# Second-layer products all 256 columns wide, with their moving operands 192 bytes beyond the weights modulo 256

## The chip, the core and the metric

The kernel runs on one core of one Trainium2 chip. The metric is the device time of one execution in microseconds, median of three runs. The core has a matrix engine (TensorE, PE in the profile, with its weight loads listed apart as PEld), VectorE (DVE), ScalarE (ACT), GpSimd (POOL) and a queue for transfers (SP). Tiles lie in on-chip memory of 128 partitions; an address below is the byte offset in a partition. Products are summed in PSUM.

## What is computed

Three stages follow each other. A gated scan over 768 steps for 4 batches and 8 heads gives 3072 rows of 256 numbers; a first layer of width 1536 with SiLU gating; a second layer of width 2048 with a squared ReLU:

```
y   = scan(x, a, B, C)                       # 3072 rows x 256
xn  = y / sqrt(mean(y*y) + 1e-6) * rms_g
r1  = (silu(xn @ w_gate) * (xn @ w_val)) @ w_out1     # 3072 x 256
h   = r1 @ w_in                              # 3072 x 2048
out = (s * relu(h)**2 + b) @ w_out           # 3072 x 256
```

## The kernel before, in words

Rows lie along the columns of tiles, features along partitions. Every full-precision number is kept as two float32r numbers, a high part and the rest (`split`, line 802: a copy on ACT that rounds, a subtraction on DVE). A product of two such pairs is three TensorE products, high x high, low weight x high, high weight x low (`three`, line 795). Each of the three names its own weights, so each comes with a weight load of 128 x 128.

The scan and the first layer share the first part of the program. The first layer goes over blocks of 384 or 512 rows (`NB`); its first block multiplies ten of its twelve feature tiles in plain float32 (`hidden1_plain`, line 849). The second layer starts at about 363 us and goes over six groups of 512 rows, each with 16 feature tiles taken in 8 pairs (`seven`, line 963). For one pair there are twelve h products: two feature tiles x two halves of the 256 inputs x three. Each has 512 columns (line 970). ACT then applies ReLU to the 512 columns of a PSUM bank and squares them; the columns are two halves of 256 rows, and the pair of features and the pair of halves go through seven products instead of eight: DVE forms sums and differences (`added`, `less`), each is split into `hi` and `lo`, and `seven_out` (line 993) makes 7 x 3 = 21 products of 256 columns with combined weights `w2c`, summed over the eight pairs into seven PSUM areas (called `acc` or `o` in the trace, according to the bank). These 21 products stand in TensorE's order two pairs behind the h products (`LAG`, line 51). After eight pairs the seven sums are put together (lines 1003 to 1025) and stored. ACT and DVE need the time of a pair for the work on the next.

The order on each engine is computed before anything is emitted: class `Plan` records every operation with an estimated duration (`price`, line 216) and its dependences (`touch`, line 182), lists them forward and backward, and emits each engine's instructions in the order found. For a float32r product it assumes n / 2.285 + 7 ns (line 231).

Where the tiles lie matters for the change. The weights `w2h` and `w2c`, the rows `x1h` and `x1l`, and `hi` and `lo` come from pools that follow each other in memory. Each buffer of these pools has a multiple of 256 bytes per partition (3072 for `w1h` and the `hi` and `lo` of `seven`, 4096 for the rows, 2048 for `w2h` and for the pool `hl`). So all of them, weights and moving operands, start at the same address modulo 256.

The buffers of the first layer's high weights, pool `wts` with 12 buffers, are used again in the second layer for `hi` and `lo`, four per pair, which repeats every three pairs.

Of the kernel before, what the change touches and what calls it, by code (L numbers as in the profile page):

```python
# [8 lines left out]
F32 = mybir.dt.float32  # L9
F32R = mybir.dt.float32r  # L10
# [9 lines left out]
P = 128  # L20
# [28 lines left out]
KEPT = max([t1 - t0 for parts in PARTS for _, t0, t1 in parts[1:]])  # L49
LAST = [max(c for c in range(NUNIT) if any(j == i for i, *_ in PARTS[c])) for j in range(NBLK)]  # L50
LAG = 2
F1 = 12
F2 = 16
PLAIN = 10
HALVES = 5
ORDER = [*range(PLAIN, F1), *range(PLAIN)]
N2 = 512
HALF = N2 // 2
DM = 256
SIZE = {F32: 4, F32R: 4, I32: 4, U32: 4, BF16: 2, I16: 2, U16: 2, I64: 8}  # L60
# [3 lines left out]
class Engine:  # L64
    def __init__(self, plan, name):
        self.plan, self.name = plan, name
# [5 lines left out]
class Plan:  # L72
# [21 lines left out]
    SWITCH = {"matmul": 0.24, "transpose": 0.15}  # L94
    LATE = 0.6
    PASSES = 3

    def __init__(self, nc):
        self.nc, self.ops, self.clock, self.pace = nc, [], 0.0, False
# [82 lines left out]
    def touch(self, op, ap, write):  # L182
        t = getattr(ap, "tensor", None)
        tag = getattr(t, "tag", None)
        if tag is None:
            return
        tag = str(tag)
        name = ap.name
        whole = "PSUM" in str(ap.space) or "DRAM" in str(ap.space)
        if name not in self.seen:  # L190
            self.seen[name] = []
            ring = self.rings.setdefault(tag, [])
            bufs = t.bufs or t.tag_meta.bufs
            self.before[name] = list(self.seen[ring[-bufs]]) if len(ring) >= bufs else []
            self.closed.update(ring[:1 - bufs] if bufs > 1 else ring)
            ring.append(name)
        for *_, o in self.before[name]:
            self.need(op, o)
        p0, p1, mask = (0, 128, self.banks(ap)) if whole else self.cover(ap)
        for w, q0, q1, m, o in self.seen[name]:  # L200
            apart = "PSUM" in str(ap.space) and o["eng"] != op["eng"]
            if (apart or (write or w) and m & mask) and q0 < p1 and p0 < q1:
                self.need(op, o)
        assert name not in self.closed, name
        self.seen[name].append((write, p0, p1, mask, op))

    def need(self, op, o):
# [137 lines left out]
    def issue(self, idle, warm):  # L345
# [13 lines left out]
        found = []  # L359
        for _ in range(self.PASSES):  # L360
            start, stop = self.forward(succs, late)
# [34 lines left out]
def scan_glu_relu2(ctx: ExitStack, tc: tile.TileContext, bc, xr, aa, cst, w1, w2, gn, sv, bv, out):  # L396
    nc = Plan(tc.nc)
    PS = bass.MemoryType.PSUM

    const = ctx.enter_context(tc.tile_pool(name="const", bufs=1))  # L400
    wts = ctx.enter_context(tc.tile_pool(name="wts", bufs=F1))
    wlo = ctx.enter_context(tc.tile_pool(name="wlo", bufs=F2))
    dram = ctx.enter_context(tc.tile_pool(name="dram", bufs=1, space=bass.MemoryType.DRAM))
    w2_p = ctx.enter_context(tc.tile_pool(name="w2", bufs=4))
# [8 lines left out]
    hl_p = ctx.enter_context(tc.tile_pool(name="hl", bufs=LAG + 1))  # L413
    res_p = ctx.enter_context(tc.tile_pool(name="res", bufs=1))
# [16 lines left out]
    warm = const.tile([P, 1], F32, name="warm")  # L431
    a_scr = dram.tile([2 * NUNIT, NH * AW], F32, name="a_scr")

    w1h = {m: wts.tile([P, 6, P], F32R, tag="w1h", name="w1h") for m in ORDER}
    w1f, w1l, w2f, w2h = {}, {}, {}, {}
    w2_sum = const.tile([P, 2, P], F32, name="w2_sum")

    def f32(t):
        return t.bitcast(F32)
# [256 lines left out]
            )  # L696

    rest = {}
    kept = const.tile([P, 2, 2, KEPT], F32, name="kept")

    def turn(units):
        for c in units:
            new_rows(BLOCK[c])
        bundled("t", units, turn_products)
        for c in units:
            tp = y_p[c % NPAIR][:, 1, 4 * R:4 * R + 2 * P].rearrange("p (k z r) -> p k z r", k=2, z=2)
            (j, t0, t1), *more = PARTS[c]
            place_rows(j, c, [tp[:, k, :, NST + t0:NST + t1] for k in range(2)])
            for j, t0, t1 in more:
                rest[j] = (c, kept[:, :, :, 0:t1 - t0])  # L710
                nc.vector.tensor_copy(out=rest[j][1], in_=tp[:, :, :, NST + t0:NST + t1])

    def turn_rest(j):
# [43 lines left out]
    def flat(t):  # L757
        return t.rearrange("p a b -> p (a b)")
# [3 lines left out]
    def words(out, src):  # L762
        nc.turns = True
        nc.sync.dma_start(out=out, in_=src)
        nc.turns = False
# [18 lines left out]
    def decode2(m):  # L784
        raw = w2_p.tile([P, 4 * P], I64, tag="w2", name="raw2")
        words(raw, w2[m])
        w2f[m] = w2f_p.tile([P, 4, P], F32, tag="w2f", name="w2f")
        decode(raw, flat(w2f[m]), 4 * P, nc.vector)
        if m:
            last = w2f[0][:, 2:4] if m == 1 else w2_sum  # L790
            nc.gpsimd.tensor_tensor(out=w2_sum, in0=last, in1=w2f[m][:, 2:4], op=ALU.add)

# [2 lines left out]
    def three(out, wh, wl, xh, xl, first, last):  # L795
        nc.pace = True
        nc.tensor.matmul(out=out, lhsT=wh, rhs=xh, start=first, stop=False)
        nc.tensor.matmul(out=out, lhsT=wl, rhs=xh, start=False, stop=False)
        nc.tensor.matmul(out=out, lhsT=wh, rhs=xl, start=False, stop=last)
        nc.pace = False  # L800
# [8 lines left out]
    o_t, x1_t, rows1 = {}, {}, {}  # L809
# [11 lines left out]
    def evac1(o, t, j):  # L821
        at, end = START[j], START[j + 1]
        for i in range(at // (2 * N2), (end - 1) // (2 * N2) + 1):
            if i not in rows1:
                rows1[i] = x1_p.tile([P, 2, 2 * N2], F32, tag="x1", name="rows1")
            lo, hi = max(at, 2 * N2 * i), min(end, 2 * N2 * (i + 1))
            nc.scalar.copy(out=rows1[i][:, t, lo - 2 * N2 * i:hi - 2 * N2 * i], in_=o[t][:, lo - at:hi - at])

    def split_rows(g):
        x1_t[g] = [w2_p.tile([P, 2, N2], F32R, tag="w2", name=f"x1{v}") for v in "hl"]  # L830
        split(rows1[g // 2][:, :, g % 2 * N2:(g % 2 + 1) * N2], *x1_t[g])

    def hidden1(j, m):
# [107 lines left out]
    def bias_products():  # L941
        ps = ps_y.tile([P, 2, 512], F32, tag="y", name="bias")
        ones = nc.nc.const_aps.tensor(1.0, (P, 2), F32)
        for t in range(2):
            nc.tensor.matmul(out=ps[:, t, 0:2], lhsT=w2_sum[:, t], rhs=ones, start=True, stop=True)
        nc.vector.tensor_scalar(out=minus_s, in0=s_sb, scalar1=-1.0, scalar2=None, op0=ALU.mult)
        for t in range(2):
            nc.vector.tensor_scalar_mul(bias_sb[:, t:t + 1], ps[:, t, 0:1], b_sb)

    def new_sums(j):  # L950
        n = HALF

# [10 lines left out]
    def seven(j, q):  # L963
        n = HALF
        (xh, xl), s = x1_t[j], []
        for i in range(2):
            m = 2 * q + i
            ps = ps_h.tile([P, 512], F32, tag="h", name="h")[:, :2 * n]
            for k in range(2):
                three(ps, w2h[m][:, 0, k], w2h[m][:, 1, k], xh[:, k], xl[:, k], k == 0, k == 1)  # L970
            t = s_p.tile([P, 2 * n], F32, tag="s", name="s")
            nc.scalar.activation(out=t, in_=ps, func=AF.Relu)
            nc.scalar.activation(out=t, in_=t, func=AF.Square)
            s.append(t.rearrange("p (s n) -> p s n", s=2))

        added = xt_p.tile([P, 3, n], F32, tag="xtl", name="added")
        less = xt_p.tile([P, 2, n], F32, tag="xth", name="less")
        hi, lo = ([wts.tile([P, 3, n], F32R, tag="w1h", name=f"{v}{k}") for k in range(2)] for v in ("hi", "lo"))
        hi2 = hl_p.tile([P, n], F32R, tag="hi", name="hi")
        lo2 = hl_p.tile([P, n], F32R, tag="lo", name="lo")  # L980
        split(s[0][:, 0], hi[1][:, 2], lo[1][:, 2])
        split(s[1][:, 1], hi2, lo2)
        nc.vector.tensor_tensor(out=added[:, 0], in0=s[0][:, 0], in1=s[1][:, 1], op=ALU.add)
        for i in range(2):
            nc.vector.tensor_tensor(out=added[:, 1 + i], in0=s[i][:, 0], in1=s[i][:, 1], op=ALU.add)
        split(added, hi[0], lo[0])
        nc.vector.tensor_tensor(out=less, in0=s[0], in1=s[1], op=ALU.subtract)
        split(less, hi[1][:, 0:2], lo[1][:, 0:2])
        parts = [(hi[1][:, 2], lo[1][:, 2]), (hi2, lo2)] + [(hi[0][:, k], lo[0][:, k]) for k in range(3)]
        parts += [(hi[1][:, k], lo[1][:, k]) for k in range(2)]  # L990
        pending.append(lambda: seven_out(j, q, parts))

    def seven_out(j, q, parts):
        n = HALF
        if q == 0:
# [31 lines left out]
    def drain(n):  # L1027
# [13 lines left out]
        out=ident, in_=ident, compare_op=ALU.not_equal, fill=1.0, base=0,  # L1041
# [3 lines left out]
    for z in range(2):  # L1045
        rows = slice(z * R, (z + 1) * R)
        nc.vector.tensor_copy(
            out=delta[rows, :, 0:CH], in_=ident[rows, None, z * R + NST:(z + 1) * R].to_broadcast([R, NH, CH])
# [3 lines left out]
    for u in range(4):  # L1052
        rows = slice(u * 32, (u + 1) * 32)
        nc.vector.tensor_copy(
            out=first_bc[rows, :, 0:NST], in_=ident[rows, None, u * 32:u * 32 + NST].to_broadcast([32, 2, NST])
# [66 lines left out]
    start = {(layer, j): i for i, (layer, j, m) in reversed(list(enumerate(plan)))}  # L1122
    marks = [(start[1, j], count[LAST[j]]) for j in range(1, NBLK)]
    for i, (layer, j, m) in enumerate(plan):
        at = i - start[layer, j]
# [101 lines left out]
```

## Time and profile before

| | us |
|---|---|
| median of 3 runs (lowest to highest) | 626.06 (625.53 to 626.33) |
| the profiled execution | 626.15 |
| its span, first to last instruction | 624.4 |
| TensorE busy | 614.7 |
| VectorE busy | 484.5 |
| ScalarE busy | 448.4 |
| GpSimd busy | 55.2 |

The profiled execution is 0.09 us above the median. The span leaves out 1.75 us ahead of the first and behind the last instruction. The granted TensorE clock was 0.999 of full speed over the span. A product's duration in the trace, such as 392 ns for 512 columns, holds its passage through the array, and the next product starts well before it ends. What a product costs is the distance from its start to the start of the next; the chain of waits shows that distance summed over a run of products.

### The profile page before, as it was taken

To read this page: it belongs to the slowest core of one execution; us is meant where nothing else is said; L and a number is where in the kernel's file an instruction comes from. 1 tells how busy PE (TensorE), PEld (TensorE's weight loads), DVE (VectorE), ACT (ScalarE), POOL (GpSimd) and SP (SyncE) were. 2 spreads that over 40 slices of the span, in tenths; PEclk is the share of its full clock that TensorE was granted. 3 is DMA by queue.
4 is the path that set the end of the run, shared out by engine and by line. 5 is a ranking of instruction groups with operands and counts; after the bars stand their busy time and mean duration, and the time that the engine had idled before them with its cause. 6 is when DMAs were issued, how large, how long until landed. Compare 5 with 4: busy or idle time off the path is not lost.

```text
span 624.4 us, 12905 instructions
## 1 busy us (share of the span) xinstructions
PE 614.7 (98%) x4937; PEld 544.2 (87%) x4937; DVE 484.5 (78%) x978; ACT 448.4 (72%) x945; POOL 55.2 (9%) x88
## 2 busy tenths in 40 slices
PE   9999999999999999999999999999999999999996
PEld 7886899999988888888889999999999999999985
DVE  7999965778856865685685678898897897987975
ACT  5797553766636653664665589898898998988984
POOL 3001100010101110101231310000000000000000
PEclk9999999999999999999999999999999999999999
DMA  6876413425514421520000000001010010010101
GB/s 220 235 238 182 125 31 65 97 64 114 127 38 99 101 69 39 122 52 1 2 2 0 1 2 1 1 12 24 1 34 1 2 35 0 10 27 1 35 0 36
DMA packets 33695, 35.01 MB, mean 56 GB/s; under 512 B 13792, under 2 KB 30048, under 8 KB 33632
## 3 DMA queue, kind: packets, MB, share of 16 engines
q1 hardware_dynamic: 32704, 33.71, 20.5%
q8 instruction: 39, 0.64, 0.4%
q10 hardware_dynamic: 928, 0.46, 0.3%
q14 instruction: 24, 0.20, 0.1%
HBM read 30.90 MB, written 3.25 MB: 55 GB/s over the span
## 4 chain that ended last, share of the span: by engine, by line
PE 95%; ACT 2%; DMA 1%; DVE 1%; issue 0%; DVEq 0%; ACTq 0%
PE h L381 53%; PE o L381 23%; PE acc L381 13%; PE y L381 5%; DMA raw<-in_w 1%; PE o L374 1%; ACT sg L381 0%; ACT xh L381 0%; ACT xn L381 0%; PE ab L381 0%; ACT e L381 0%; DVE m L381 0%; DVE res L381 0%; ACT xth L381 0%; DVE a_sb L381 0%
## 5 line engine op out<-in xcount | busy, mean ns | idle before, releaser
L381 ACT CAST hi<-s 128x256 fp32r<-128x256 f32 (+2 forms) x170 | 80.1, 474 | 73.0 <-DVE s L381 71.2
L381 ACT ACTIVATE s<-h 128x512 f32<-128x512 f32 (+1 forms) x170 | 97.3, 572 | 33.6 <-PE h L381 30.2
L381 PE MATMUL h<-x1h,w2h 128*128 128x512 f32 x384 | 119.4, 392 | 0.0
L381 DVE TENSOR_TENSOR lo<-s,hi 128x256 fp32r<-128x256 f32 (+2 forms) x170 | 87.3, 514 | 30.2 <-ACT hi L381 27.2
L381 PE MATMUL h<-xth,w1h 128*128 128x384 f32 (+1 forms) x296 | 109.0, 368 | 0.5 <-DVE s L381 0.5
L381 PE MATMUL h<-xth,w1l 128*128 128x384 f32 (+1 forms) x296 | 107.7, 364 | 0.0
L381 PE MATMUL h<-xtl,w1h 128*128 128x384 f32 (+1 forms) x296 | 107.1, 364 | 0.0
L381 PE MATMUL acc<-hi,w2c 128*128 128x256 f32 x448 | 82.5, 283 | 0.0
L381 PEld LDWEIGHTS h<-x1h,w2h 128*128 128x128 f32 x384 | 69.2, 189 | 12.0
L381 PE MATMUL h<-x1l,w2h 128*128 128x512 f32 x192 | 74.7, 389 | 0.0
L381 DVE TENSOR_TENSOR s<-h,s 128x384 f32<-128x384 f32 (+1 forms) x74 | 45.7, 618 | 36.1 <-PE h L381 33.5
L381 PEld LDWEIGHTS acc<-hi,w2c 128*128 128x128 f32 x448 | 71.7, 191 | 2.3
L381 DVE TENSOR_TENSOR added<-s 128x256 f32<-128x256 f32 x144 | 56.6, 421 | 13.6 <-ACT s L381 12.8
L381 PE MATMUL acc<-lo,w2c 128*128 128x256 f32 x224 | 63.4, 283 | 0.0
L381 PEld LDWEIGHTS h<-xth,w1h 128*128 128x128 f32 x296 | 55.6, 188 | 7.4 <-DVE s L381 1.0
L381 ACT ACTIVATE s<-s 128x512 f32<-128x512 f32 x96 | 60.3, 633 | 1.8
L381 PEld LDWEIGHTS h<-xth,w1l 128*128 128x128 f32 x296 | 55.6, 188 | 6.1 <-issue 0.2
L381 PEld LDWEIGHTS h<-xtl,w1h 128*128 128x128 f32 x296 | 55.5, 188 | 5.7 <-issue 0.2
L381 PE MATMUL o<-hi,w1h 128*128 128x384 f32 (+1 forms) x148 | 53.9, 364 | 0.0
L381 PE MATMUL o<-lo,w1h 128*128 128x384 f32 (+1 forms) x148 | 53.9, 365 | 0.0
L381 PE MATMUL o<-hi,w1l 128*128 128x384 f32 (+1 forms) x148 | 53.8, 363 | 0.0
L381 DVE TENSOR_TENSOR lo<-added,hi 128x768 fp32r<-128x768 f32 x48 | 45.9, 957 | 1.0 <-ACT hi L381 0.7
(101 smaller groups left out, 1074.6 us busy)
## 6 DMA issues: line engine op xcount, KB each, us to landing
raw<-in_w SPq DMA_DIRECT2D x12, 768.0 KB, 5.7
raw<-in_w SPq DMA_DIRECT2D x16, 512.0 KB, 3.4
a_sb<-a_scr SPq DMA_DIRECT2D x28, 196.0 KB, 3.7
xh<-in_xr SPq DMA_DIRECT2D x60, 48.0 KB, 1.8
raw_bc<-in_bc SPq DMA_DIRECT2D x56, 32.0 KB, 3.8
raw_bc<-in_bc SPq DMA_DIRECT2D x112, 16.0 KB, 1.7
out_t<-res SPq DMA_DIRECT2D x10, 96.0 KB, 1.9
first_bc<-in_bc SPq DMA_DIRECT2D x8, 62.0 KB, 5.0
```

The lines of the kernel that those rows point to most:

```text
L374: self.nc.tensor.matmul(out=idle, lhsT=ones, rhs=ones, start=not fills, stop=True, skip_group_check=True)
L381: getattr(engine, op["fn"])(*op["args"], **op["kw"])
```

## The change

Two things are changed, in the second layer alone.

First, each h product of 512 columns becomes two of 256. The six products of the first 256 columns come first, then the six of the second 256, into the two halves of the same PSUM bank. One pair then has 24 h products and 21 others, all of 256 columns and each with its weight load.

Second, the moving operands are put 48 numbers (192 bytes) further: the rows `x1h` and `x1l` by a longer tile (1088 numbers), the single `hi2` and `lo2` by tiles of 304 numbers, and the other `hi` and `lo` by cutting them out of one long tile, `ring`, at 48 + 768 k. The ring is also the home of the twelve high weights of the first layer, which stay where they were relative to everything else. The weights keep their places, so every moving operand of the second layer starts 192 bytes beyond its weights modulo 256. `RECUT` drops old records of the ring from the planner's list when a range is written again. To pay for the longer tiles, `w2_sum` (which adds up all output weights for the bias) and `kept` (rows put aside between blocks) leave the constants and share a tile of the pool `res`, whose only buffer holds results later.

```
-    wts = ctx.enter_context(tc.tile_pool(name="wts", bufs=F1))
+    wts = ctx.enter_context(tc.tile_pool(name="wts", bufs=1))
...
+    ring = wts.tile([P, F1 * 6 * P + P], F32R, tag="ring", name="ring")
+    w1h = {m: ring[:, k * 6 * P:(k + 1) * 6 * P].rearrange("p (a b) -> p a b", b=P) for k, m in enumerate(ORDER)}
+    cuts = iter(range(F2 // 2 * 6 * 4))
+    def cut():
+        at = OFF + next(cuts) % F1 * 3 * HALF
+        return ring[:, at:at + 3 * HALF].rearrange("p (a b) -> p a b", b=HALF)
...
+            t = res_p.tile([P, 2 * P + 4 * KEPT], F32, tag="res", name="aside")
...
     def split_rows(g):
-        x1_t[g] = [w2_p.tile([P, 2, N2], F32R, tag="w2", name=f"x1{v}") for v in "hl"]
+        x1_t[g] = [
+            w2_p.tile([P, 2 * N2 + 64], F32R, tag="w2", name=f"x1{v}")[:, OFF:OFF + 2 * N2].rearrange(
+                "p (k n) -> p k n", k=2
+            ) for v in "hl"
+        ]
...
-            for k in range(2):
-                three(ps, w2h[m][:, 0, k], w2h[m][:, 1, k], xh[:, k], xl[:, k], k == 0, k == 1)
+            for at in (0, n):
+                cols = slice(at, at + n)
+                for k in range(2):
+                    three(ps[:, cols], w2h[m][:, 0, k], w2h[m][:, 1, k], xh[:, k, cols], xl[:, k, cols],
+                          k == 0 and not at, k == 1 and at > 0)
...
-        hi, lo = ([wts.tile([P, 3, n], F32R, tag="w1h", name=f"{v}{k}") for k in range(2)] for v in ("hi", "lo"))
-        hi2 = hl_p.tile([P, n], F32R, tag="hi", name="hi")
-        lo2 = hl_p.tile([P, n], F32R, tag="lo", name="lo")
+        hi, lo = ([cut() for k in range(2)] for v in range(2))
+        hi2, lo2 = (hl_p.tile([P, OFF + n], F32R, tag=v, name=v)[:, OFF:] for v in ("hi", "lo"))
```

TensorE's order in the middle of a pair of the first group, before: the last six of the twelve h products, then the first of the 21.

```order
L381 MATMUL h<-x1h,w2h 128x512 x2
L381 MATMUL h<-x1l,w2h 128x512
L381 MATMUL h<-x1h,w2h 128x512 x2
L381 MATMUL h<-x1l,w2h 128x512
L381 MATMUL acc<-hi_984,w2c 128x256 x2
L381 MATMUL acc<-lo_986,w2c 128x256
L381 MATMUL acc<-hi,w2c 128x256 x2
L381 MATMUL acc<-lo,w2c 128x256
```

The same place after the change: the last six of 24, then all of the 21.

```order
L385 MATMUL h<-x1h,w2h 128x256 x2
L385 MATMUL h<-x1l,w2h 128x256
L385 MATMUL h<-x1h,w2h 128x256 x2
L385 MATMUL h<-x1l,w2h 128x256
L385 MATMUL acc<-ring,w2c 128x256 x3
L385 MATMUL acc<-hi,w2c 128x256 x2
L385 MATMUL acc<-lo,w2c 128x256
L385 MATMUL acc<-ring,w2c 128x256 x15
```

The sequence of h products, then the 21, is the same; twelve rows of 256 columns stand where six of 512 stood.

ScalarE's order over the turn from one pair to the next in the same group, before (`s<-h` is the ReLU, `s<-s` the square, the casts make the high parts):

```order
L381 CAST hi<-s 128x256
L381 CAST hi_984<-less 128x512
L381 CAST hi_983<-added 128x768
L381 ACTIVATE s<-h 128x512
L381 ACTIVATE s<-s 128x512
L381 ACTIVATE s<-h 128x512
```

The same turn after the change:

```order
L385 CAST hi<-s 128x256
L385 CAST ring<-less 128x512
L385 ACTIVATE s<-h 128x512
L385 CAST ring<-added 128x768
L385 ACTIVATE s<-s 128x512
L385 ACTIVATE s<-h 128x512
```

Here one ReLU has moved ahead of one cast; some twenty such exchanges of neighbours are spread over the second layer on ACT and half as many on DVE, and no instruction is added or taken away on either.

## Rows read from the trace of the kernel before

**Rows 1.** The page: busy time of each engine, and the chain's shares by engine.

```profile
PE 614.7 (98%) x4937; PEld 544.2 (87%) x4937; DVE 484.5 (78%) x978; ACT 448.4 (72%) x945; POOL 55.2 (9%) x88
...
PE 95%; ACT 2%; DMA 1%; DVE 1%; issue 0%; DVEq 0%; ACTq 0%
```

**Rows 2.** Chain of waits, second layer: start us, us, what.

```profile
363.11 2.76 PE h L381 x12
365.87 1.06 PE o L381 x6
...
500.20 2.51 PE acc L381 x21
502.71 2.75 PE h L381 x12
...
615.33 2.89 PE o L381 x24
...
618.31 1.27 DVE res L381 x3
```

**Rows 3.** Chain of waits, three runs of first-layer products.

```profile
41.39 1.30 PE h L381 x8
...
43.34 2.58 PE h L381 x8
...
344.39 2.08 PE h L381 x12
```

**Rows 4.** Timeline around one product and its neighbour's weight load: start, us, engine.

```profile
443.49 0.28 PE L381 MATMUL acc<-lo,w2c 128*128 128x256 f32 x1
443.49 0.31 PEld L381 LDWEIGHTS acc<-hi,w2c 128*128 128x128 f32 x2
```

**Rows 5.** Timeline of TensorE over one pair's twelve h products.

```profile
428.91 0.63 PE L381 MATMUL h<-x1h,w2h 128*128 128x512 f32 x2
...
429.61 0.62 PE L381 MATMUL h<-x1h,w2h 128*128 128x512 f32 x2
...
430.30 0.62 PE L381 MATMUL h<-x1h,w2h 128*128 128x512 f32 x2
...
430.98 0.62 PE L381 MATMUL h<-x1h,w2h 128*128 128x512 f32 x2
...
431.66 0.40 PE L381 MATMUL o<-hi,w2c 128*128 128x256 f32 x2
```

**Rows 6.** Timeline of TensorE behind small products of the scan, first layer.

```profile
251.83 0.40 PE L381 MATMUL o<-hi,w1l 128*128 128x512 f32 x1
252.07 0.40 PE L381 MATMUL o<-lo,w1h 128*128 128x512 f32 x1
252.31 0.40 PE L381 MATMUL h<-xth,w1h 128*128 128x512 f32 x1
```

**Rows 7.** Timeline of ScalarE where it has no pause, first pairs of the second layer.

```profile
372.24 0.60 ACT L381 ACTIVATE s<-h 128x512 f32<-128x512 f32 x1
372.72 0.62 ACT L381 CAST hi<-less 128x512 fp32r<-128x512 f32 x1
373.24 0.63 ACT L381 ACTIVATE s<-s 128x512 f32<-128x512 f32 x1
...
374.25 0.84 ACT L381 CAST hi<-added 128x768 fp32r<-128x768 f32 x1
374.97 0.64 ACT L381 ACTIVATE s<-s 128x512 f32<-128x512 f32 x1
375.50 0.71 ACT L381 CAST hi<-s 128x256 fp32r<-128x256 f32 x2
376.11 0.41 ACT L381 CAST w2c<-sums 128x256 fp32r<-128x256 f32 x1
```

**Rows 8.** Busy time by stretch: us, PE, PEld, DVE, ACT, POOL, PEclk, DMA share, GB/s.

```profile
363.11:384.48 21.37, 21.37 (x120) 18.86 (x120) 19.06 (x41) 20.37 (x43) 1.06 (x2) 1.00 0.00 1
384.48:500.20 115.72, 115.72 (x728) 104.93 (x728) 98.03 (x193) 104.92 (x193) 0.00 (x0) 1.00 0.05 10
```

More of the change, by code (lines that the diff above doesn't have):

```diff
@@ L57 @@
 N2 = 512
+OFF = 48
 HALF = N2 // 2
@@ L96 @@
     PASSES = 3
+    RECUT = ("ring",)
     def __init__(self, nc):
@@ L204, in touch @@
         assert name not in self.closed, name
+        if write and name in self.RECUT:
+            self.seen[name] = [e for e in self.seen[name] if e[3] & ~mask or e[1] < p0 or e[2] > p1]
         self.seen[name].append((write, p0, p1, mask, op))
@@ L432, in scan_glu_relu2, with put_aside @@
     a_scr = dram.tile([2 * NUNIT, NH * AW], F32, name="a_scr")
-    w1h = {m: wts.tile([P, 6, P], F32R, tag="w1h", name="w1h") for m in ORDER}
-    w1f, w1l, w2f, w2h = {}, {}, {}, {}
-    w2_sum = const.tile([P, 2, P], F32, name="w2_sum")
+    ring = wts.tile([P, F1 * 6 * P + P], F32R, tag="ring", name="ring")
[4 more added lines that the diff above has]
+        return ring[:, at:at + 3 * HALF].rearrange("p (a b) -> p a b", b=HALF)
+    w1f, w1l, w2f, w2h = {}, {}, {}, {}
+    aside = {}
+    def put_aside():
+        if not aside:
+            t = res_p.tile([P, 2 * P + 4 * KEPT], F32, tag="res", name="aside")
+            aside["sum"] = t[:, 0:2 * P].rearrange("p (a b) -> p a b", b=P)
+            aside["kept"] = t[:, 2 * P:].rearrange("p (a b c) -> p a b c", a=2, b=2)
+        return aside
     def f32(t):
@@ L698, in scan_glu_relu2 @@
     rest = {}
-    kept = const.tile([P, 2, 2, KEPT], F32, name="kept")
     def turn(units):
@@ L709, in turn @@
             for j, t0, t1 in more:
-                rest[j] = (c, kept[:, :, :, 0:t1 - t0])
+                rest[j] = (c, put_aside()["kept"][:, :, :, 0:t1 - t0])
                 nc.vector.tensor_copy(out=rest[j][1], in_=tp[:, :, :, NST + t0:NST + t1])
@@ L789, in decode2 @@
         if m:
+            w2_sum = put_aside()["sum"]
             last = w2f[0][:, 2:4] if m == 1 else w2_sum
@@ L944, in bias_products @@
         for t in range(2):
-            nc.tensor.matmul(out=ps[:, t, 0:2], lhsT=w2_sum[:, t], rhs=ones, start=True, stop=True)
+            nc.tensor.matmul(out=ps[:, t, 0:2], lhsT=aside["sum"][:, t], rhs=ones, start=True, stop=True)
         nc.vector.tensor_scalar(out=minus_s, in0=s_sb, scalar1=-1.0, scalar2=None, op0=ALU.mult)
```

## The prediction

> **What bounds the kernel now.** I read the page first. TensorE is busy for 98% of the span and the chain of waits lies on it for 95% [rows 1], so only a change in TensorE's own time, or a new wait of TensorE, can move the end. The reader is to see next, in the chain, how regular the second layer is: from 363.11 us on it is one row of h products and one of the 21 others after the other, twelve in 2.75 us and 21 in 2.51 us, without a piece of any other engine until the last product at 615.33 + 2.89 = 618.22 us [rows 2]. A pair costs 2.75 + 2.51 = 5.26 us, and 6 groups x 8 pairs make 48 x 5.26 = 252.5 us. As a check, 618.22 - 363.11 = 255.1 us, less two runs of six first-layer products at 1.06 us that stand in between, leaves 253.0.
>
> Then I asked what one product costs beyond its columns. A product of 256 columns takes 2.51 / 21 = 119.5 ns from start to start; a settled h product of 512 takes 0.68 / 3 = 226.7 ns (the last two steps of [rows 5]); a first-layer product of 384 takes 2.08 / 12 = 173.3 ns [rows 3]. 256 more columns cost 107 ns, which is 2.4 columns per ns, the full clock (granted share 1.00 [rows 8]). What is left is the same each time: 120 - 106.7 = 13.3 ns, 173.3 - 160 = 13.3, 226.7 - 213.3 = 13.4. So today a product costs its columns / 2.4 plus 13.3 ns, whatever its length. Plain float32 products, which also load weights each time and whose tiles start at the same address modulo 256, don't pay this: eight records of 192 columns take 1.30 us and eight of 384 take 2.58 us [rows 3], 162.5 and 322.5 ns, so 160 ns per 192 columns and 2.5 ns left over. The 13.3 ns are therefore no fixed price of changing weights.
>
> Two more views show what they depend on. A weight load starts at the same 0.01 us as the product before the one it serves [rows 4], so the two readings of on-chip memory, moving operand and next weights, begin together. And the 13.3 ns are not constant: behind the change from 256 to 512 columns three h products take 0.70, then 0.69, then 0.68 and 0.68 us [rows 5]; behind the small products of the scan, products of 512 columns take 0.24 us [rows 6], 213.3 + 26.7, twice the usual remainder, and settle again. Something whose size depends on how the two readings stand to each other, and which locks in, fits this better than a fixed cost. With operands and weights at the same address modulo 256, that standing is what the change moves.
>
> **The change, part by part.**
>
> *More, shorter h products.* 576 products of 512 columns become 1152 of 256, with 576 more weight loads. With the 1008 others that makes 2160 products of 256 columns, 45 per pair. If the remainder stays at 13.3 ns, a pair costs 45 x 120 = 5.40 us, 0.14 more than now. The remainder at which the change breaks even is 5.26 / 45 - 106.7 = 116.9 - 106.7 = 10.2 ns.
>
> *The 192 bytes.* No fp32r product in the trace has its operand elsewhere than at its weights modulo 256, so this is bounded by rows: from above by the 26.7 ns of rows 6 (133.3 ns per product), from below by no remainder at all (106.7 ns). The nearest price in between is that of the float32 products, 2.5 ns [rows 3], whose weight loads run beside them too. I take it: 109.2 ns per product, 45 x 109.2 = 4.914 us per pair, 48 x (5.26 - 4.914) = 16.6 us saved. I take this end rather than 13.3 because the remainder moves with the standing of the two readings [rows 5, 6] and is absent where the operand is read at half the rate [rows 3]. At the other ends the pair costs 4.80 us (22.1 us saved) or 6.00 us (35.5 us lost).
>
> The Trainium skill, in "TensorE: Matmul & The Clock Gate", section "Back-to-back issue gap", puts the gap at N / 2.4 + 2.5 ns. By it a product of 256 columns costs 109.2 ns already before the change. The trace has 119.5 ns there and 162.5 for 160 ns of columns in float32, so the rule holds for the second and leaves out what is at stake in the first; by the rule alone a pair would cost 2.59 + 2.29 = 4.88 us before and 4.91 after.
>
> *ACT and DVE.* They have as many instructions as before; a few neighbours change places, as the rows on ScalarE's order show. The question is whether they keep up with a pair of 4.914 us. Between 384.48 and 500.20 us there are 22 pairs, with ACT busy 104.92 us and DVE 98.03 [rows 8], 4.77 and 4.46 us per pair. This bounds their need from above, since the end of one instruction overlaps the start of the next. From below: steps of ACT without a pause are 0.48 us for a ReLU, 0.53 for a square, 0.52, 0.72 and about 0.30 for the casts of 512, 768 and 256 columns [rows 7], so 2 x 0.48 + 2 x 0.53 + 0.52 + 0.72 + 2 x 0.30 = 3.86 us per pair, before the work at the end of a group. Both are below 4.914: in the steady part TensorE stays the bound. At five group ends ACT's and DVE's extra work falls into two pairs, and a ReLU that is late holds up the next h products, since there are two PSUM banks for them; I put 0.1 us on each, 0.5 us, between 0 and 5 x 0.35.
>
> *The first pairs.* From 363.11 to 384.48 us ACT is busy 20.37 of 21.37 us [rows 8], because it still makes the weights of the last two pairs beside its usual work. That holds four pairs, and ACT needs up to 5.09 us for each. The 4 x 0.35 us that TensorE would save there turn into waits for ACT for the most part; I take 1.0 of the 1.4 us.
>
> *The ring and the shared tile.* A cast into the ring waits for products of three pairs earlier, as with the twelve buffers. DVE gets some 40 more separate wait instructions, about one per pair; what they wait for stood ahead of the h products that DVE is working on, so they cost their issue alone, in an engine with slack. I put nothing on this; its bound is the slack of DVE, so nothing again unless DVE reaches 4.9 us. The bias sum and `kept` take over the place of the first block's rows after it is done, and are done themselves before results are written there: nothing.
>
> Sum: 626.15 - 16.6 + 1.0 + 0.5 = 611.05 us in the terms of the profiled execution, whose time stands 0.09 us above the median of the runs. I predict **611 us**. The end behind the last product (final sums and store, from 618.22 us) is unchanged.
>
> **The rivals.**
>
> *The address changes nothing* (slower). If the 13.3 ns belong to float32r itself, an operand read at full rate whose weights are loaded beside it, every one of the 576 extra products adds them. For it: the remainder is the same at 256, 384 and 512 columns, although the readings overlap for quite different shares of the product. Against it: rows 5 and 6, where it is not the same. Place: all 48 pairs; price: 5.40 - 5.26 = 0.14 us each, 6.7 us, so 632.9 us. It decides from a remainder of 10.2 ns on.
>
> The Trainium skill speaks for this rival: "TensorE: Matmul & The Clock Gate", section "Step-by-step: what each phase is for", says that TensorE has two independent read ports and that loading the next weights takes nothing from the running product. By that rule the place of the operand cannot matter, and only the added products count; that the remainder varies in this trace is what it doesn't explain.
>
> *Half of it goes.* The two readings meet twice in a load (256 bytes come round twice in 512) and only one meeting is avoided. Remainder 6 to 9 ns, say 7.9: 45 x 114.6 = 5.157 us, 48 x 0.10 = 4.9 us saved, about 621.5 us.
>
> *A second wait.* The new standing locks in at 26.7 ns as in rows 6: 48 x 0.74 = 35.5 us more, 661.7 us. For it there are only a few products at a time; none of them stays so.
>
> **How the numbers follow.** Chances: the remainder falls to about 2.5 ns, 0.58 (own range 607.5 to 615, from no remainder with the same waits to 4.5 ns of it); half of it goes, 0.13; it ends near break-even, 0.05; the address changes nothing, 0.20; a second wait, 0.04. Differences under 0.2%, 1.25 us, can't be told from none with this kernel. Faster: 0.58 + 0.13 = 0.71; same 0.05; slower 0.20 + 0.04 = 0.24. To leave out no more than 2 in 10 the range must reach the case at 632.9: 607 to 633.5.
>
> **What will show it.** In the chain after, rows of 24 h products and 21 others: 2.62 and 2.29 us if I am right, 2.88 and 2.52 if the address does nothing. First-layer rows of twelve products of 384 stay at 2.08 us in either case. ACT and DVE should show about the same busy time in a shorter layer, and TensorE's waits for ACT or DVE should stay within the first four pairs and the group ends. If products take 109 ns but the layer is shorter by less than 12 us, the step on ACT and DVE was wrong; if they take 120, the step on the 192 bytes.

## The result, and the profile after

The changed kernel takes **619.25 us** (median of 20 executions) where the kernel before takes 626.03 us (20 executions beside them). The ratio is 0.9897, 95% interval 0.988 to 0.9914: faster, by 6.8 us, less than half of the 15 us forecast. Fourteen of its executions lie at 618.15 to 619.87 us; the other six, of which the ratio leaves out five, lie at 627.4 to 630.2, above all twenty of before, so that the mean of all twenty is only 4.0 us below that of before (622.04 and 626.05). The experiments come back to these six. The profiled execution took 618.92 us, that of before 626.15.

The page of the changed kernel, busy time and the chain's shares, to be held against [rows 1]:

```profile
PE 606.4 (98%) x5513; PEld 559.9 (91%) x5513; DVE 483.2 (78%) x978; ACT 445.5 (72%) x945; POOL 55.3 (9%) x88
...
PE 91%; DMA 3%; DVE 2%; ACT 2%; issue 1%; SPq 0%; DVEq 0%; ACTq 0%
```

TensorE has 576 instructions more and is busy 8.3 us less. DVE and ACT have as many as before and about the same busy time. TensorE's share of the chain falls from 95 to 91%. DMA's rises from 1 to 3%, ahead of the second layer, and DVE's from 1 to 2%; a later view shows a stretch of some 13 us at the turn to the second layer where the chain now runs through ACT and DVE.

The chain of waits in the second layer (start us, us, what), which answers to [rows 2]:

```profile
376.73 2.72 PE h L385 x24
379.45 2.38 PE acc L385 x21
381.83 2.72 PE h L385 x24
...
606.23 2.04 PE acc L385 x18
608.27 2.73 PE o L385 x24
...
611.10 1.27 DVE res L385 x3
```

A pair costs 2.72 + 2.38 = 5.10 us instead of 5.26, and no pair behind the third takes longer. Both rows give the same product: 2.72 / 24 = 2.38 / 21 = 113.3 ns. For the 21 others that is 120.0 - 113.3 = 6.7 ns less each, 0.14 us per pair. The h products bring nothing: two of 113.3 ns cost what one of 512 columns cost, 226.7 ns [rows 5]. The rest of the 0.16 us is the turn from 256 to 512 columns, which is gone. 48 x 0.16 = 7.7 us.

Busy time by stretch (us, PE, PEld, DVE, ACT, POOL, PEclk, DMA share, GB/s), one pair and the 22 after it, which answers to [rows 8]:

```profile
376.57:381.67 5.10, 5.10 (x47) 5.10 (x46) 4.59 (x11) 5.01 (x11) 0.00 (x0) 1.00 0.01 3
381.67:493.87 112.20, 112.20 (x992) 112.20 (x991) 97.20 (x192) 103.07 (x191) 0.00 (x0) 1.00 0.05 11
```

In the first regular pair ACT is still busy 5.01 of 5.10 us. Behind it 112.20 / 22 = 5.10 us per pair again, with ACT at 4.68 and DVE at 4.42: TensorE never waits for them. The granted clock is 1.00, as before.

The 7.7 us saved in all the pairs are 0.9 more than the 6.8 of the medians (the two profiled executions differ by 7.2). About as much is lost at the start of the layer. TensorE's timeline there (start us, us, engine, line, operation, in brackets the idle time before it and who ended it):

```profile
370.25 0.39 PE L385 MATMUL h<-x1h,w2h 128*128 128x256 f32 x2
...
372.96 0.28 PE L385 MATMUL acc<-ring,w2c 128*128 128x256 f32 x1
373.08 0.50 PE L385 MATMUL bias<-const-float32-1.0,aside 128*128 128x2 f32 x4
373.44 0.48 PE L385 MATMUL acc<-ring,w2c 128*128 128x256 f32 x2
373.76 0.40 PE L385 MATMUL acc<-hi,w2c 128*128 128x256 f32 x2
...
374.11 0.52 PE L385 MATMUL acc<-ring,w2c 128*128 128x256 f32 x3
375.11 1.62 PE L385 MATMUL acc<-ring,w2c 128*128 128x256 f32 x12 [0.49 <-DVE sb L385]
376.57 0.39 PE L385 MATMUL h<-x1h,w2h 128*128 128x256 f32 x2
```

And the chain of waits ahead of it, where DVE is late:

```profile
373.44 0.33 DVE lo L385
373.78 0.34 DVE w2c L385
374.11 0.60 DVE ring L385
374.71 0.27 DVE sb L385 x2
374.98 0.14 issue
375.11 1.62 PE acc L385 x12
```

In the first run of 21, TensorE stands still for 0.49 us, until DVE has copied the bias (`sb`) and so given a PSUM bank back. From its first h product, at 370.25 us, to the next pair's at 376.57 this pair takes 6.32 us: 5.10 as any other, 0.36 for the four bias products (373.08 to 373.44), which before has in its third pair too, and 0.86 that are lost around them. From 361.9 us to here the chain goes through ACT and DVE, which still make weights beside their usual work.

### The profile page after: what moved, and what is told of

The parts are those of the page before. It is cut to its first block, busy times and chain, and to the rows that moved or that the text cites. A ratio compares the mean times of both kernels' runs of the same rounds, so it can differ in the third digit from the quotient of the medians.

```text
span 617.1 us, 14100 instructions
## 1 busy us (share of the span) xinstructions
PE 606.4 (98%) x5513; PEld 559.9 (91%) x5513; DVE 483.2 (78%) x978; ACT 445.5 (72%) x945; POOL 55.3 (9%) x88
## 4 chain that ended last, share of the span: by engine, by line
PE 91%; DMA 3%; DVE 2%; ACT 2%; issue 1%; SPq 0%; DVEq 0%; ACTq 0%
PE h L385 52%; PE o L385 22%; PE acc L385 12%; PE y L385 5%; DMA raw<-in_w 2%; DMA a_sb<-a_scr 1%; ACT s L385 1%; DMA first_bc<-in_bc 0%; SPq L385 0%; DVE w1f L385 0%; ACT ring L385 0%; DVE e L385 0%; ACT xh L385 0%; DVE m L385 0%; DVE res L385 0%
## 5 line engine op out<-in xcount | busy, mean ns | idle before, releaser
L385 PE MATMUL h<-x1h,w2h 128*128 128x256 f32 x768 | 132.9, 276 | 0.0
L385 PE MATMUL h<-xth,ring 128*128 128x384 f32 (+1 forms) x296 | 108.8, 367 | 1.2 <-DVE s L385 1.2
L385 PE MATMUL h<-xtl,ring 128*128 128x384 f32 (+1 forms) x296 | 107.0, 364 | 0.0
L385 PE MATMUL h<-x1l,w2h 128*128 128x256 f32 x384 | 106.0, 276 | 0.0
L385 PE MATMUL acc<-ring,w2c 128*128 128x256 f32 x576 | 78.7, 276 | 0.5 <-DVE sb L385 0.5
L385 PEld LDWEIGHTS h<-x1l,w2h 128*128 128x128 f32 x384 | 72.1, 188 | 0.0
L385 PEld LDWEIGHTS acc<-ring,w2c 128*128 128x128 f32 x576 | 71.4, 188 | 0.7 <-issue 0.7
L385 PEld LDWEIGHTS h<-xth,ring 128*128 128x128 f32 x296 | 55.6, 188 | 7.8 <-DVE s L385 1.5
L385 PEld LDWEIGHTS h<-xtl,ring 128*128 128x128 f32 x296 | 55.5, 188 | 5.7 <-issue 0.2
L385 PE MATMUL o<-hi,ring 128*128 128x384 f32 (+1 forms) x148 | 54.0, 365 | 0.0
```

What stands on the lines that cost most here:

```text
L385: getattr(engine, op["fn"])(*op["args"], **op["kw"])
```

## The experiments

Two theories stood at the start. **A**: what a product costs beyond its columns is set by the distance of its operand from the weights modulo 256, and at 192 bytes it is smaller. **B**: the distance does nothing, and the gain comes from a stream of one length only.

**One part alone: the split.** All products of 256 columns, everything at distance 0.

```
-OFF = 48
+OFF = 0
```

> The changed kernel with its 24 h products of 256 columns, but with every moving operand back at its weights' address modulo 256. Theory A (the place of the operand relative to its weights sets what a product costs beyond its columns: 13.3 ns at 0 bytes, 6.7 ns at 192): a product costs 120 ns, a pair 45 x 120 = 5.40 us, the kernel about 626.0 + 6.7 = 633 us. Theory B (a stream of equal lengths sets it, the address is idle): a product stays at 113.3 ns, a pair at 5.10 us, the kernel at 619 us.

Measured: 632.87 us, before 626.18 beside it; ratio 1.0096 (1.007 to 1.0121). The chain over one pair (`acc` and `o` together are the 21):

```profile
473.70 2.88 PE h L385 x24
476.58 1.08 PE acc L385 x9
477.66 1.44 PE o L385 x12
```

2.88 / 24 = 2.52 / 21 = 120.0 ns, a pair of 5.40 us. The split by itself costs 6.7 us, exactly what the rival "the address changes nothing" had worked out for it. B falls: one length in a stream is not enough.

**The other part alone: the 192 bytes.** The changed kernel with h products of 512 columns again.

```
-            for at in (0, n):
-                cols = slice(at, at + n)
-                for k in range(2):
-                    three(ps[:, cols], ...
+            for k in range(2):
+                three(ps, w2h[m][:, 0, k], w2h[m][:, 1, k], xh[:, k], xl[:, k], k == 0, k == 1)
```

> The changed kernel with its operands 192 bytes beyond the weights, but with h products of 512 columns as before. Theory A, with 6.7 ns at any length: 12 x 220 + 21 x 113.3 = 5.02 us per pair, about 615 us, faster than the change. Theory B: 5.26 us per pair, 626 us. A third, that the place helps products of 256 columns alone: 12 x 226.7 + 21 x 113.3 = 5.10 us, 619 us, no difference from the change.

Measured: 626.19 us; ratio 0.9993 (0.998 to 1.0006), no change. The chain over one pair, and over the last sums:

```profile
471.16 2.79 PE h L385 x12
473.95 1.06 PE acc L385 x9
475.01 1.41 PE o L385 x12
...
613.25 2.04 PE acc L385 x18
```

The time is that of before, as theory B had it, but not for B's reason: the products have changed. The sums fell to 2.47 / 21 = 117.6 ns, and the h products rose to 2.79 / 12 = 232.5 ns. So 192 bytes are good for 256 columns and bad for 512, and the two cancel. In the last row, where only 256-column products follow each other, one costs 113.3 ns. The two parts bring nothing or a loss alone, and 6.8 us together: the 512-column product at its best costs two of 113.3, so only with the split do the h products go along at 192 bytes.

**A sweep over distances**, one for each of the six groups of rows, first with all products of 256 columns (0, 64, 128, 160, 192, 224 bytes), then with h of 512 (0, 32, 64, 96, 128, 192). At the turn of two groups a few numbers of a cut are overwritten by the next group's, so a part of the output is something else in these two.

```
+OFFS = (0, 16, 32, 40, 48, 56)
-        at = OFF + next(cuts) % F1 * 3 * HALF
+        at = OFFS[j] + next(cuts) % F1 * 3 * HALF
```

> The changed kernel, all 256 columns, with another distance in each of the six groups of 512 rows: 0, 64, 128, 160, 192 and 224 bytes. Theory A: 5.40 us per pair in the first group and 5.10 in the fifth, and the others at levels of their own, between 45 x 106.7 = 4.80 and 45 x 133.3 = 6.00 us; a distance with 2.5 ns left over would show as 4.91. Theory B: 5.10 us in all six groups.

> As the sweep before, with h products of 512 columns, at distances of 0, 32, 64, 96, 128 and 192 bytes. Theory A: the 21 products of 256 columns take 2.52 us at 0 and 2.38 at 192, and twelve h products 2.72 and 2.64; where the remainder is a property of the distance alone, both lengths show the same remainder at each distance. Theory B: 2.51 and 2.75 us in all groups. If the place helps the short products alone, h stays at 2.72 to 2.75 in all groups while the 21 others change.

Measured, one execution each (627.83 and 625.62 us), settled pair of each group, from the start of its first h product to the start of the next pair's:

| bytes | 0 | 32 | 64 | 96 | 128 | 160 | 192 | 224 |
|---|---|---|---|---|---|---|---|---|
| all 256, us | 5.400 | | 5.300 | | 5.340 | 5.280 | 5.100 | 5.320 |
| h of 512, us | 5.260 | 5.247 | 5.127 | 5.323 | 5.279 | | 5.267 | |

The price does follow the distance, and 192 is the best for 256 columns. But where the group at 192 begins and its products still alternate with those of the group before, one run of its twelve h products took 117.6 ns each (from 535.40 us of that trace) and the next, with the same rows, 113.3 (from 537.89).

**Products by themselves.** TensorE alone, all of the kernel's own work left out, eight tiles of operands at distances of 0 to 224 bytes, runs of 36 to 60 products of one kind.

```
+        for k, x in enumerate(xs):
+            at = 8 * k
+            products(x, at, 256, 128, 60)
+            products(x, at, 512, 128, 36)
+            products(x, at, 256, 128, 60)
+            products(x, at, 384, 128, 36)
+            ...
+            products(x, at, 256, 64, 48)
```

> No layer at all: TensorE alone, streams of equal float32r products with nothing beside them, for eight distances of the operand beyond the weights (0 to 224 bytes in steps of 32; the tile is named after the step, x_zero to x_seven). For each distance 60 products of 256 columns, 36 of 512, 60 of 256 again, 36 of 384, and behind a pause 48 of 256 with weights of 64 columns. Theory A1 (the remainder is the operand's reading meeting the load's once per 256 bytes of load, and the distance decides how many meetings cost): 120 ns at distance 0 and 113.3 at 192 for 256 columns; with weights of 64 columns, half as many bytes, about half the remainder, 113.3 and 109 to 110 ns. Theory A2 (6.7 ns is the floor of float32r, and the place adds to it): 113.3 ns is the least at any distance, and weights of 64 columns change nothing at 192. That a state outlives its cause (B): the second 60 products of 256 columns, entered from 512, differ from the first 60 at the same distance, by up to 5 ns each.

Measured, ns from one start to the next over the second half of each run:

| bytes | 256 columns | 256 behind 512 | 512 | 384 | 256, weights of 64 columns |
|---|---|---|---|---|---|
| 0 | 120.0 | 120.0 | 226.7 | 173.3 | 113.3 |
| 32 | 116.7 | 116.7 | 233.3 | 176.7 | 119.1 |
| 64 | 117.8 | 113.3 | 228.9 | 173.3 | 116.7 |
| 96 | 120.0 | 120.0 | 233.3 | 176.6 | 116.7 |
| 128 | 118.7 | 120.0 | 232.0 | 176.2 | 116.7 |
| 160 | 118.7 | 117.3 | 234.4 | 173.3 | 117.1 |
| 192 | 117.8 | 113.3 | 233.3 | 173.3 | 119.0 |
| 224 | 118.2 | 118.4 | 233.3 | 173.3 | 116.7 |

With no other engine at work the kernel's prices return, 120.0 and 226.7 at distance 0 and 113.3 at 192, so no other engine's traffic makes them. No entry for 256 columns is under 113.3, the floor of A2. A1 falls: with weights of 64 columns at 192 bytes it had 109 to 110 ns and A2 no change, and the run has 119.0. One remainder for all lengths, which theory A had in the second experiment, is gone too: at 192 bytes it is 6.7 ns for 256 columns and 20.0 for 512. And at 64 and 192 bytes the same product has two prices, 117.8 and 113.3, by what ran ahead of it. In all the runs the weights keep their place and the operand moves; whether its distance from the weights counts, or its own place modulo 256, they don't tell apart.

**The cheapest mix by this table**, distance 64 with h of 512 columns.

```
-OFF = 48
+OFF = 16
```

(on top of the kernel with the 192 bytes alone)

> The changed kernel with h products of 512 columns again and operands 64 bytes beyond the weights instead of 192, since the third group of the sweep on 512 columns took 5.127 us per pair. If the distance alone decides (A): 48 x (5.26 - 5.127) = 6.4 us less than before, about 619.8 us, as fast as the change without its added products. If that pair depended on the group ahead of it (B): 5.22 to 5.30 us per pair, 624 to 628 us.

Measured: 624.34 us, ratio 0.995 (0.9923 to 0.9976). The chain over one pair of an execution of 624.84 us:

```profile
476.11 2.76 PE h L385 x12
478.87 1.06 PE acc L385 x9
479.93 1.41 PE o L385 x12
```

The sums stand at 2.47 / 21 = 117.6 ns: the dearer price. Three of its ten executions took 618.8 to 619.9 us. That is what the 5.127 us of the sweep's group at 64 bytes would give instead of 2.76 + 2.47 = 5.23 (48 x 0.106 = 5.1 us less), but none of these three was profiled.

**What the 6.7 ns are.** TensorE alone again, seven lengths, weights of 32 and of 128 columns.

```
+        for k in (0, 2, 6):
+            for cols, lengths in ((32, (128, 192, 256, 320, 384, 448, 512)),
+                                  (128, (192, 256, 320, 448, 512))):
+                for n in lengths:
+                    products(x, at, n, cols, 36)
```

> TensorE alone, runs of 36 float32r products of one length, with six alternating sets of weights, operands at 0, 64 and 192 bytes beyond the weights modulo 256; the kernel's own output is left out. It asks what the 6.67 ns are that a product of 256 columns keeps at 192 bytes (113.33 - 106.67). H1, a meeting of the weight load with the operand's reading: with weights of 32 columns the remainder falls to 3.3 ns or less at every length and distance (256 columns in 110.0 or less). H2, a fixed floor of float32r: 6.67 ns at every length at its best distance, with weights of 32 as of 128 columns: 192 columns 86.7, 256 113.3, 320 140.0, 384 166.7, 448 193.3, 512 220.0 ns. H3, a tax in proportion to the columns (1/16 of them): 192 columns 85.0, 256 113.3, 320 141.7, 384 170.0, 448 198.3, 512 226.7 ns whatever the weights. At distance 0 the three agree only in that 256 columns take 120.0 and 512 take 226.7 with 128 columns of weights.

Measured, chain of waits, runs of 36: weights of 32 columns with 256 columns at distance 0; weights of 128 with 192 and with 256 at distance 0; the last with 256 at 192.

```profile
15.74 4.09 PE m L98 x36
...
48.08 4.05 PE m L98 x36
...
52.38 4.35 PE m L98 x36
...
190.75 4.15 PE m L98 x36
```

Settled, these are 113.3, 111.7, 120.0 and 113.3 ns (a run's first product takes longer). The least that any distance and weight width gave, here and in the table above, is 59.8, 88.1, 113.3, 143.3, 173.3, 200.0 and 226.7 ns for 128, 192, 256, 320, 384, 448 and 512 columns, so beyond the columns / 2.4 there remain 6.5, 8.1, 6.7, 10.0, 13.3, 13.3 and 13.4 ns. H1 falls: weights of a quarter of the width leave the 6.7 ns of 256 columns. H2 falls as stated, since the rest doubles towards 512 columns; H3 falls, since it gives 3.3 ns for 128. What fits best is some 6.7 ns for each 256 columns begun, with 320 in between; why, stays open. The upper half does go with narrow weights at distance 0: there 256 columns cost 120.0 with weights of 128 columns and 113.3 with 32 or 64. But that is no rule for other distances: at 192 bytes weights of 64 columns cost 119.0, more than those of 128. Whether a wide load disturbs the operand's reading, or only takes nearly as long as the product does (with weights of 128 columns even 192 columns cost 111.7), these runs don't tell apart.

**The sums alone at 192 bytes**, h with 512 columns at distance 0, each at the distance that is best for it.

```
-            w2_p.tile([P, 2 * N2 + 64], ...)[:, OFF:OFF + 2 * N2].rearrange(
+            w2_p.tile([P, 2 * N2 + 64], ...)[:, 0:2 * N2].rearrange(
```

(on top of the kernel with the 192 bytes alone)

> One part alone: the moving operands of the 21 sums products lie 192 bytes beyond the weights, the h products keep 512 columns and distance 0. Theory C (what a product costs is set by its own length and its own distance, and at 192 bytes there are two self-holding prices, 113.3 and 117.8 ns, chosen on entry): h 12 x 226.7 = 2.72, the others 21 x 113.3 = 2.38 and some 0.03 for the turn, pair 5.125 us, 48 x 0.135 = 6.5 us less than before, 619.5 us at the lower price; 21 x 117.8 = 2.47, pair 5.22, about 624 us at the upper. Theory B (only one unbroken stream of one length reaches the low price): 117.8 or more in every pair but the last, 624 us or above.

Measured: 623.21 us, ratio 0.9958 (0.9943 to 0.9973). The chain over one pair, and the last sums:

```profile
474.39 2.72 PE h L385 x12
477.11 1.06 PE acc L385 x9
478.17 1.41 PE o L385 x12
...
611.56 2.84 PE o L385 x24
```

h is at 226.7 ns and the sums at 2.47 / 21 = 117.6 in every pair, 5.19 us. This is theory C's dearer branch, with h at once at its settled price, so a little below its 624. The last run of sums stays dear too, 2.84 / 24 = 118 ns, where B had let it fall.

**The way in.** Groups of 24 products of one kind, at 192 and then at 64 bytes; only what stands ahead differs.

```
+            for n in (1, 2, 3, 4, 5, 6):
+                fill(n)
+                products(x, at, 256, P, 24)
+            for n in (3, 4, 5, 6):
+                products(xs[0], 0, 384, P, n)
+                products(x, at, 256, P, 24)
```

(and the same behind 3 to 6 products of 512, and behind a wait for VectorE that ends in one product of 2 columns)

> TensorE alone: groups of 24 float32r products of 256 columns whose operand lies 192 (then 64) bytes beyond the weights modulo 256, all with the same six sets of weights; only what stands ahead of a group differs: 1 to 6 small bf16 products, 3 to 6 products of 384 columns or 3 to 6 of 512 at distance 0, or a wait for a VectorE copy of 128 to 256 columns. The kernel's own output is left out. Theory D (at these two distances the price is a state that the way in chooses): groups of one and the same kind of product settle at 113.3 ns in some and at 117.8 ns in others, and stay there to their end; at 192 bytes both occur. Theory E (operand, weights and distance fix the price): every group at 192 settles at one price within six products, 113.3 ns, and every group at 64 at one price, 117.8 ns, whatever stands ahead.

Measured at 192 bytes, chain of waits behind small bf16 products (`idle`):

```profile
12.79 2.79 PE m L98 x24
15.58 0.18 PE idle L94 x3
15.76 2.88 PE m L98 x24
18.64 0.25 PE idle L94 x4
18.89 2.88 PE m L98 x24
21.77 0.31 PE idle L94 x5
22.08 2.79 PE m L98 x24
```

Timeline of TensorE behind three products of 384 and behind three of 512 columns, the last products' passage included:

```profile
27.86 0.69 PE L98 MATMUL m<-x_zero,w 128*128 128x384 f32 x3
28.39 2.88 PE L98 MATMUL m<-x_six,w 128*128 128x256 f32 x24
...
41.89 0.86 PE L98 MATMUL m<-x_zero,w 128*128 128x512 f32 x3
42.58 2.99 PE L98 MATMUL m<-x_six,w 128*128 128x256 f32 x24
```

Same products, same addresses: 2.88 or 2.99 us, 113.3 or 117.8 ns settled, and each group keeps its price to its end. Behind 384 columns at distance 0 all four groups took 113.3, behind 512 all four took 117.8, behind small products four of six took 113.3, behind a wait two of six. D holds at 192 bytes; at 64 all twenty groups took 117.8, as E has it there. The way in is more than a length: 36 products of 512 columns at 192 bytes instead of 0 led to 113.3 (table above, "256 behind 512"). It fits the kernels: in the one above, the sums come behind 512 columns at distance 0 and are dear in every pair.

**The wait at the start taken out.** The changed kernel, with the bias products marked (`pace`) so that the planner lists them where the program names them, at the start of the first layer's last block (326.4 us in the trace), and no longer within the first sums.

```
         for t in range(2):
+            nc.pace = True
             nc.tensor.matmul(out=ps[:, t, 0:2], lhsT=aside["sum"][:, t], ...
+            nc.pace = False
```

> The changed kernel with one edit: the few products that prepare the bias stand at the start of the first layer's last block and no longer within the first run of sums. If the gap of some 0.8 us at 372.9 to 375.1 us comes from those products waiting for DVE's copy, it goes, and the time is 618.5 us, 0.7 below the changed kernel. If the first pairs are paced by ACT and DVE anyway, another wait takes its place and the time stays within 0.3 us of the changed kernel's 619.25; the pairs after 376 us keep 5.10 us in either case, if they enter at the lower price.

Measured: 618.23 us, ratio to before 0.9875 (0.9858 to 0.9891). The chain over the third and fourth pair, and its last pieces:

```profile
371.28 2.72 PE h L385 x24
374.00 2.38 PE acc L385 x21
376.38 2.72 PE h L385 x24
...
607.02 0.97 DVE ring L385
...
608.41 2.84 PE o L385 x24
```

The gap at 375 us is gone: this pair takes 5.10 us instead of 6.32. Of these 1.2 us, 0.36 are the bias products themselves, which are now paid earlier. In the profiled execution (619.07 us) the rest doesn't reach the end either: the second layer's first h product starts 0.9 us later than in the changed kernel (363.59 instead of 362.71 us), and another wait has come, of 0.22 us for DVE at 608.0 us, in the last sums.

**The same kernel once more**, for the executions near 629 us.

> The changed kernel with the bias products moved ahead of the first layer's last block, executed some more times. If the changed kernel's occasional times near 629 us come from the way TensorE enters the stream of 256-column products, and that way in varies only because of its wait for VectorE at 372.9 to 375.1 us, all of these executions lie at 617.5 to 619.5 us; if the way in varies for other reasons, about 3 in 10 lie near 628 us (45 x 4.45 ns x 48 = 9.6 us more).

Measured: 618.86 us, ratio 0.9888 (0.9872 to 0.9905). The chain's last products:

```profile
608.23 2.74 PE o L385 x24
```

What a wait can do to the price is to be seen here. The late wait for DVE comes in this execution too (0.20 us), the sums ahead of it are 113.3 ns apart in both, and the 24 products behind it cost 2.74 / 24 = 114 ns here and 2.84 / 24 = 118 in the execution before. One kernel so takes either price at the same place. In the changed kernel the wait at 375 us went the other way: the products between the bias and the wait are 117 to 118 ns apart, those behind it settle at 113.3 and keep it to the end.
The eight executions of the two runs lie at 617.82 to 619.45 us, none near 629. With 6 in 20 as in the changed kernel, eight in a row without one would come about 1 time in 17 (0.7 to the eighth). So that the wait made the way in vary is likely, and not shown; nor was an execution near 629 us profiled, though 45 x 4.5 ns x 48 = 9.7 us more fits it. Against the changed kernel's lower executions the gain is not larger than the intervals.

## Why the forecast missed

- *Bound, and the form of the cost*: right for this kernel. TensorE stayed the bound, and columns / 2.4 plus a remainder of 13.3 ns describes before. But "whatever its length" holds only for the lengths that the kernel has: at distance 0 with weights of 128 columns the remainder is 31.7 ns for 192 columns (111.7) and 20.0 for 448 (206.7).
- *More, shorter h products*: right to the digit. Without the offset a pair costs 45 x 120 = 5.40 us and the kernel 632.87 us, against 632.9 worked out.
- *The 192 bytes*: **this step failed, by the size of its term.** "The nearest price in between is that of the float32 products, 2.5 ns", 109.2 ns per product, 16.6 us saved. The remainder is 6.7 ns, 113.3 per product, 7.7 us saved. The mechanism, that the place of the operand moves the remainder, was right for 256 columns; for 512 the same place costs 6.6 ns more (233.3 instead of 226.7). But a plain float32 product has another price law: no float32r run of any length, distance or weight width came under 6.5 ns. The price from [rows 3] was that of another kind of product, and the bounds of 0 and 26.7 ns were so wide that this choice decided the whole forecast. The rival "half of it goes" had both the size (6 to 9 ns) and nearly the time (621.5 us): of 13.3 ns 6.7 go and 6.7 stay. That was luck as far as its reason goes: if one of two meetings in a load is left, weights of half the bytes should halve what remains (A1 above, 109 to 110 ns), and at 192 bytes weights of 64 columns cost 119.0. Why 6.7 ns stay is open.
- *Against the Trainium skill*: by the formula in "TensorE: Matmul & The Clock Gate", section "Back-to-back issue gap", which it gives for single products, 256 columns would cost 109.2 ns, an estimate. The runs have 113.3 to 120.0, and the measurement decides. The Trainium skill says on the same page, section "Step-by-step: what each phase is for", that TensorE has two independent read ports and that loading the next weights takes no read bandwidth from the running product. That the load therefore leaves the product's cost alone, as the prediction read it, isn't so here: at distance 0, 256 columns cost 113.3 ns with weights of 32 columns and 120.0 with 128.
- *ACT and DVE in the steady part*: no wait at 5.10 us per pair. Whether they would hold 4.91 was not put to the test. At the ends of the groups the 0.5 us did not come.
- *The first pairs*: 1.0 us forecast, 0.9 lost, in part by luck. Forecast were waits for ACT over four pairs; found was one stop, at the return of the bias bank by DVE, behind a chain of 13 us of which ACT has 7.1. The saving there was also put too high: the stretch of [rows 8] holds five rows of h products and two of the 21 others, which at 109.2 ns save 5 x 0.13 + 2 x 0.22 = 1.1 us and not 1.4.
- *A second wait*: it does exist, but as 117.8 ns instead of 113.3, not as 133.
- *The range*: the favoured case's own lower end doesn't follow from its terms. No remainder with the same waits is 626.15 - 22.1 + 1.5 = 605.6 us, not 607.5.

## What to carry to other kernels

A float32r product with new weights each time has a price that depends on its length, on the width of the weights, on where the operand lies (here its address modulo 256, with the weights at 0) and on what ran just ahead. Measure them together: here each part of the change alone was worth nothing or a loss, and both together 1%. Where a cost has never been seen for this kind of instruction, a price from another kind is a bound and no estimate; ten microseconds of TensorE alone on the chip would have shown 113 to 118 ns and not 109. And look for two levels among the executions: a stream of equal products can keep, for hundreds of microseconds, a price that its first products happened upon.

## Not expected of the hardware

- At 192 bytes products of 256 columns have two prices that hold themselves, 113.3 and 117.8 ns. Three to six products of 384 columns at distance 0 ahead lead to the first, of 512 at distance 0 to the second, a wait to either.
- For 512 columns distance 0 is the best of eight (226.7 ns, else 228.9 to 234.4); for 256 columns with weights of 128 it is, with 96 bytes, the worst (120.0).
- With weights of 128 columns, 192 columns cost 111.7 ns, hardly less than 256 (113.3 at best); with weights of 32 they cost 88.1.
